# Unread matrix products of 512 columns in place of 128, three more groups of them, and a weight piece issued between the decayed keys of units 2 and 3

## The chip, the cores and the metric

The kernel runs on one core of a Trainium2 chip. Five engines work on their own instruction streams and wait for each other through semaphores: TensorE (PE, matrix products; its weight loads are listed apart as PEld), VectorE (DVE), ScalarE (ACT), GpSimd (POOL) and SyncE (SP). Transfers between memory and the chip are issued by SP, ACT or POOL and run on 16 DMA engines that they share. The metric is the device time of one execution in microseconds; lower is better.

## The reference

A lightning-attention step with a decay per head is followed by a two-layer network with a leaky activation. Four sequences, 8 heads, 768 positions, 64 dimensions a head; the network has 512 inputs, 2048 hidden units and 3072 tokens. In blocks of positions:

```python
intra = (q_b @ k_b.T * Dmask) @ v_b
inter = (q_b * lam_pow) @ kv_state
out   = intra + inter
kv_state = lam_block * kv_state + (k_b * rev_pow).T @ v_b

h = x @ w_in
g = max(h, 0) + alpha * min(h, 0)
y = g @ w_out
```

All inputs and the output are float32; the kernel computes the products in float16 with float32 accumulation.

## The kernel before, in words

The tokens are cut into six chunks `c` of 512 (two sequences by 256 positions). A chunk's attention is done in four **units** (`bi` of two sequences, `hh` of two halves of the heads), numbered through: units 0 to 3 belong to chunk 0. The order of every engine's instructions is written out by hand as a long list of calls (L766 to L1159); no scheduler moves anything. Each engine executes its own calls in that order. PE's stream starts with the list's first call to `fill`.

The steps of one unit `n`, with the engine that does each:

- `cast` (L411) and `key_decayed` (L432) read the raw key tile: a float16 copy, and the keys times their decay, two operations each. The letter names the engine (A for ACT, V for DVE, G for POOL).
- `turn` (L446): 12 transposes on PE into the PSUM tile `tp`, which has a single buffer (tag `tk`). `turned` (L464) copies `tp` to `qkT` on ACT or DVE; the next `turn` needs that copy done.
- `decayed` (L478) multiplies the turned queries by their decay, giving `qdT`.
- `cluster(old, new)` (L500) is one dense run on PE: products of the old unit's `qdT` with the state R (L532), 16 scores `s` of the new unit (L580), the old unit's outputs from `sm` and `v` (L552), and 16 state products of the new unit (L597).
- `masked` (L608) multiplies scores by the decay mask on DVE, giving `sm`. `aged` (L673) on POOL and `state` (L653) on ACT or DVE advance the state R.
- `out_of` (L632) copies the finished output to `xT`, the input of the network.

The network's steps are `up` (L694: four products with columns of `w_in` into a PSUM bank), `below` (L707, a relu on ACT into `m`), `gate` (L712, DVE combines `m` and the bank into `g`) and `down` (L726). Three PSUM banks take turns (slots 0, 1, 2); an `up` into a slot waits until the gate before it has read that slot.

`fill(n)` (L376) issues n products of a constant 128x128 tile with itself into slot 2. Nothing reads them; they keep PE at work where its next input isn't there yet. There are eight calls, 122 products in all: 50, 4, 6, 2, 28, 16, 2, 14 (in the order of the list), each 128 columns wide, and the last of them ends before 20 us.

`load_win(c0, n)` (L115) has POOL issue the transfer of n columns of `w_in`, cast to float16 on the way. The piece of columns 1024 to 1535 is issued after `decay_mask(0)` and before the decayed keys of units 2 and 3. The `up` steps 8 to 11 of chunk 0 read it.

Of the kernel before, what the change touches and what calls it, by code (L numbers as in the profile page):

```python
# [11 lines left out]
def kernel(  # L12
# [16 lines left out]
    nc = tc.nc  # L29
    ctx.enter_context(tc.manual_schedule())  # L30
    fp32 = mybir.dt.float32
# [14 lines left out]
    CH = 2 * W  # L46
# [11 lines left out]
    ps = ctx.enter_context(tc.tile_pool(name="ps", bufs=1, space=bass.MemoryType.PSUM))  # L58
# [56 lines left out]
    def load_win(c0, n):  # L115
        nc.gpsimd.dma_start(
            out=w_in_sb[:, :, ds(c0, n)],
            in_=moe_w_in[:, ds(c0, n)].rearrange("(g p) f -> p g f", p=128),
        )
# [34 lines left out]
    filler = const.tile([128, 128], fp16, name="filler")  # L154
# [82 lines left out]
    def mask_of(hl, hh):  # L237

        m = dmask[:, hl, ds(2 * hh, 2)]
        x = [list(y) for y in m.ap]  # L240
        return bass.AP(tensor=m.tensor, offset=m.offset, ap=[x[0], x[1], [64, 2], [1, L]])
# [10 lines left out]
    def mask_log(hp):  # L252

        m = MK[hp] = bank(hp % 2, "mk_ps")
        nc.tensor.matmul(
            m[:, 0:384].rearrange("p (h x) -> p h x", h=2),
            lhsT=ident,
            rhs=drop.unsqueeze(1).to_broadcast([128, 2, 192]),
            start=True,
            stop=False,  # L260
            skip_group_check=True,
        )
        for hl in range(2):
            h = 4 * (hp // 2) + hp % 2 + 2 * hl
            log = parts[:, h : h + 1]
            for lhsT, rhs in ((log.to_broadcast([128, L]), col16[:, 0:192]), (row16, log.to_broadcast([128, 192]))):
                nc.tensor.matmul(  # L267
                    m[:, ts(hl, 192)],
                    lhsT=lhsT,
                    rhs=rhs,  # L270
                    start=False,
                    stop=(lhsT is row16),
                    skip_group_check=True,
                )
# [8 lines left out]
    def key_logs():  # L283
        nc.vector.tensor_tensor(
            out=klog,
            in0=loglam.unsqueeze(2).to_broadcast([128, H, 2]),
            in1=rev_f.unsqueeze(1).to_broadcast([128, H, 2]),
            op=ALU.mult,
        )
# [76 lines left out]
    def bank(slot, name):  # L366
        return ps.tile([128, CH], fp32, tag=f"b{slot}", name=name)

    def slopes(slot):
        at = bank(slot, "at_ps")  # L370
        nc.tensor.transpose(at[:, 0:NF], alpha_sb, ident32)
        nc.vector.tensor_scalar(
            out=oma, in0=at[:, 0:NF], scalar1=-1.0, scalar2=1.0, op0=ALU.mult, op1=ALU.add
        )

    def fill(n):  # L376

        t = bank(2, "op_fill")
        for _ in range(n):
            nc.tensor.matmul(t[:, 0:128], lhsT=filler, rhs=filler, start=True, stop=True)  # L380


# [15 lines left out]
    def engine(x):  # L398
        return nc.vector if x == "V" else nc.gpsimd

    def view(t, hh):
        return t[:, ds(4 * hh, 4), :].rearrange("p h (e d) -> p e h d", e=2)
# [8 lines left out]
    def cast(n, x, eng):  # L411
        c, bi, hh = units[n]
        t = T.setdefault(n, {})
        if (c, bi) in Q16 and x == "q":
            out = view(rows16(x, c, bi), hh)
        elif (c, bi) in Q16:
            out = t["k16"] = half_pool.tile([128, 2, 4, D], fp16, tag="k16", name="k16", bufs=4)
        else:
            if "qk16" not in t:
                t["qk16"] = half_pool.tile([128, 2, 2, 4, D], fp16, tag="qk16", name="qk16")  # L420
            out = t["qk16"][:, int(x == "k")]
        if (c, bi) in Q16 and x == "q":
            copy_on(eng, out, view(raws[c, bi, x], hh))
        else:

            copy_on(
                eng,
                out.rearrange("p e s d -> p s e d"),
                raws[c, bi, x][:, ds(4 * hh, 4), :].rearrange("p (hl hp) ed -> p hp hl ed", hp=2),
            )  # L430

    def key_decayed(n, eng="G"):  # L432
        c, bi, hh = units[n]
        kr = view(raws[c, bi, "k"], hh)
        kdec = half_pool.tile([128, 2, 4, D], fp16, tag="kdec", name="kdec", bufs=4)
        for e in range(2):
            decay = kdecay[:, ds(4 * hh, 4), e] if c < FIRST else nkdecay[:, ds(4 * hh, 4)]
            engine(eng).tensor_tensor(  # L438
                out=kdec[:, e],
                in0=kr[:, e],  # L440
                in1=decay.unsqueeze(2).to_broadcast([128, 4, D]),
                op=ALU.mult,
            )
        T.setdefault(n, {})["kdec"] = kdec
# [163 lines left out]
    def masked(n, hl=None):  # L608
        t = T[n]
        hh = units[n][2]  # L610
        if hl is not None:
            t.setdefault("sm", {})[hl] = sm_pool.tile([128, 2, 2, L], fp16, tag=f"sm{hl}", name=f"sm{hl}")
            nc.vector.tensor_tensor(  # L613
                out=t["sm"][hl],
                in0=t["s"][:, hl].rearrange("p (h x j) -> p h x j", h=2, x=2),
                in1=mask_of(hl, hh),
                op=ALU.mult,
            )
        else:

            t["sm"] = sm_pool.tile([128, 2, 2, L], fp16, tag="sm0", name="sm0")
            nc.vector.tensor_tensor(
                out=t["sm"],
                in0=t["s"][:, :, 0 : 4 * N].rearrange("p l (e x) -> p l e x", e=2),
                in1=nmask[:, ds(4 * hh, 4)]
                .rearrange("p (l h) j -> p l (h j)", l=2)
                .unsqueeze(2)
                .to_broadcast([128, 2, 2, 2 * N]),
                op=ALU.mult,
            )  # L630
# [13 lines left out]
    def follows(n, a):  # L644

        c, bi, hh = units[n]
        step = L // N if c < FIRST else 1
        b, i = 2 * (c % 2) + bi, 4 * (c // 2) + a * step
        if (b, hh, i + step) not in R:
            state_tile(b, hh, i + step)  # L650
        return R.get((b, hh, i)), R.get((b, hh, i + step))

    def state(n, a):  # L653
        before, then = follows(n, a)
        c, bi, hh = units[n]
        if then is None:
            return
        if c >= FIRST:
            for hp in range(2):
                nc.vector.scalar_tensor_tensor(  # L660
                    out=then[:, hp, :],
                    in0=before[:, hp, :],
                    scalar=nrdecay[:, 2 * hh + hp : 2 * hh + hp + 1],
                    in1=T[n]["kv"][a % 2][:, a // 2, hp, :],
                    op0=ALU.mult,
                    op1=ALU.add,
                )
        elif before is None:
            nc.scalar.activation(then, T[n]["kv"][a][:, 0], AF.Copy)  # L669
        else:  # L670
            nc.vector.tensor_tensor(out=then, in0=T[n]["kv"][a][:, 0], in1=T[n]["old", a], op=ALU.add)  # L671

    def aged(n, a):  # L673

        before, then = follows(n, a)
        if then is None:
            return
        hh = units[n][2]
        x = T.setdefault(n, {})["old", a] = half_pool.tile([128, 2, D], fp32, tag=f"old{a}", name=f"old{a}", bufs=4)
        nc.gpsimd.tensor_tensor(  # L680
            out=x,
            in0=before,
            in1=rdecay[:, ds(2 * hh, 2)].unsqueeze(2).to_broadcast([128, 2, D]),
            op=ALU.mult,
        )
# [8 lines left out]
    def up(c, f, bi, slot):  # L694
        n = CH if bi is None else W
        h_ps = HP[c, f, bi] = bank(slot, "h_ps")
        for gi in range(NHP):
            x = XT[c][:, gi]
            nc.tensor.matmul(  # L699
                h_ps[:, 0:n] if bi is None else h_ps[:, 0:n].rearrange("p (e j) -> p e j", e=2),  # L700
                lhsT=w_in_sb[:, gi, ts(f, 128)],
                rhs=x.rearrange("p e b j -> p (e b j)") if bi is None else x[:, :, bi, :],
                start=(gi == 0),
                stop=(gi == NHP - 1),
            )
# [84 lines left out]
    load16("v", 0, 1)  # L790
    slopes(1)
    key_logs()
    mask_log(2)
    cast(0, "k", "V")
    load_win(0, 256)
# [25 lines left out]
    aged(0, 1)  # L821
    turn(1)
    decay_mask(0)
    load_win(1024, 512)
    state(0, 1)
    fill(28)
    turned(1, "A")
    masked(0, 0)
    key_decayed(2, "G")
    masked(0, 1)  # L830
    cast(2, "k", "A")
    decayed(1, "V")
# [40 lines left out]
    state(3, 0)  # L873
    gate(0, 1, 0)
    aged(3, 1)
    cluster(3, None)
    load_win(1536, 512)
    state(3, 1)
    up(0, 2, 0, 2)
    out_of(3, "A")  # L880
    up(0, 3, 0, 0)
# [408 lines left out]
```

## Time and profile before

| What | us |
|---|---|
| median of three runs | 220.22 (219.63 to 220.26) |
| the profiled execution, its own time | 219.79 |
| its span, first to last instruction | 218.0 |
| DVE busy | 126.9 |
| ACT busy | 111.4 |
| POOL busy | 97.4 |

The profile is one execution. A line names the source line, the engine, the operation, the tile it writes and the tiles it reads, and the count; "idle before" is how long the engine stood still before it, with what ended the wait. "issue" stands for a wait that nothing in the profile ended. A product's recorded end is modelled, and products overlap in PE's pipeline, so the distance from start to start tells more than a single length. The chain of waits goes back from the last instruction, at each step to what released it.

### The profile page before, as it was taken

The page shows a single profiled execution, that of the slowest core. Times are in us where ns is not written, and L with a number is a line of the kernel's source. Part 1 is how long each engine was busy: PE and PEld are TensorE (multiplying, and loading weights), DVE is VectorE, ACT ScalarE, POOL GpSimd, SP SyncE. Part 2 cuts the span into 40 slices and gives each one's busy share as a digit, 9 for nine tenths or more (in the row PEclk, how much of TensorE's full clock was granted, in tenths as well). Part 3 has the DMA queues.
Part 4 walks back from the last instruction along what each step waited for, and adds up shares of the span by engine and source line. Part 5 has one row for each costly group of instructions (what it writes and reads, how often), then busy time and mean ns, then how long its engine had stood idle before and what let it go on. Part 6 is the DMA issues. An engine that isn't in the chain of part 4 may idle for free.

```text
span 218.0 us, 5901 instructions
## 1 busy us (share of the span) xinstructions
PE 209.7 (96%) x2463; PEld 112.9 (52%) x2463; DVE 126.9 (58%) x260; ACT 111.4 (51%) x209; POOL 97.4 (45%) x154
## 2 busy tenths in 40 slices
PE   8888899899999999999999999999999999999993
PEld 8677544656765545454444444444444444444452
DVE  3988786776787786554766666646755254444000
ACT  4762775834666565546565555555445434443121
POOL 7874797655988680875597352720200000000000
PEclk9999999999999999999999999999999999999999
DMA  4999899999998398499369998227011011101212
GB/s 117 248 193 226 195 164 182 202 210 198 308 218 214 74 226 93 96 186 155 87 64 220 192 229 133 69 80 70 29 51 48 6 46 48 48 8 43 96 52 94
DMA packets 71195, 28.45 MB, mean 130 GB/s; under 512 B 52080, under 2 KB 68224, under 8 KB 71168
## 3 DMA queue, kind: packets, MB, share of 16 engines
q0 software_dynamic: 26592, 8.65, 35.6%
q1 hardware_dynamic: 40800, 13.11, 31.0%
q10 hardware_dynamic: 3776, 6.31, 8.7%
q8 instruction: 19, 0.31, 0.6%
q14 instruction: 8, 0.07, 0.1%
HBM read 27.28 MB, written 6.29 MB: 154 GB/s over the span
## 4 chain that ended last, share of the span: by engine, by line
PE 91%; ACT 2%; DVE 2%; issue 2%; POOL 2%; ACTq 0%; POOLq 0%
PE h_ps L699 37%; PE o_ps L732 32%; PE o_ps L754 6%; PE acc L532 3%; PE s L580 2%; PE op_fill L380 2%; PE acc L552 2%; PE tp L460 2%; PE tp L455 1%; PE acc L597 1%; ACT qkT L392 1%; PE mk_ps L267 1%; ACT xT L392 1%; POOL vh L83 0%; ACT m L710 0%
## 5 line engine op out<-in xcount | busy, mean ns | idle before, releaser
L722 DVE SCALAR_TENSOR_TENSOR g<-m,oma,h_ps 128x512 f16<-128x512 f32 (+1 forms) x106 | 73.0, 696 | 64.1 <-ACT m L710 62.8
L699 PE MATMUL h_ps<-xT,w_in_sb 128*128 128x512 f16 (+1 forms) x424 | 96.7, 359 | 0.5 <-DVE g L722 0.2
L710 ACT ACTIVATE m<-h_ps 128x512 f32<-128x512 f32 (+1 forms) x106 | 58.8, 556 | 56.3 <-PE h_ps L699 54.7
L732 PE MATMUL o_ps<-w_out_sb,g 128*128 128x512 f16 x320 | 81.2, 379 | 0.0
L699 PEld LDWEIGHTS <-w_in_sb 128*128 128x128 f16 x424 | 39.6, 98 | 40.6 <-issue 1.4
L732 PEld LDWEIGHTS <-g 128*128 128x128 f16 x320 | 30.9, 98 | 35.8
L743 ACT ACTIVATE o_sb<-o_ps 128x512 f32<-128x512 f32 (+2 forms) x25 | 14.5, 580 | 18.8 <-PE o_ps L754 11.0
L613 DVE TENSOR_TENSOR sm<-s,dmask 128x512 f16<-128x512 f32 x32 | 21.2, 683 | 1.8 <-PE s L580 1.8
L392 ACT ACTIVATE xT<-acc 128x512 f16<-128x512 f32 x22 | 13.1, 597 | 16.5 <-PE acc L552 9.4
L680 POOL TENSOR_TENSOR old<-R,rdecay 128x128 f32<-128x128 f16 x24 | 9.6, 408 | 26.5 <-DVE R L671 16.0
L438 POOL TENSOR_TENSOR kdec<-kraw,kdecay 128x256 f16<-128x256 f32 x30 | 18.5, 645 | 0.6 <-ACT kdecay L292 0.5
L488 POOL TENSOR_TENSOR qdT<-qkT,nqdecay 128x512 f16<-128x512 f16 x8 | 9.4, 1169 | 20.8 <-DMA qkT<-qk 17.7
L488 POOL TENSOR_TENSOR qdT<-qkT,qdecay 128x512 f16<-128x512 f16 (+1 forms) x12 | 12.0, 1003 | 4.8 <-DVE qkT L394 3.1
L754 PE MATMUL o_ps<-w_out_sb,g 128*128 128x512 f16 (+2 forms) x80 | 14.0, 336 | 0.0
L532 PE MATMUL acc<-qdT,R 64*64 64x64 f16 (+1 forms) x216 | 10.9, 217 | 0.9 <-ACT R L669 0.7
L380 PE MATMUL op_fill<-filler 128*128 128x128 f16 x122 | 10.3, 252 | 1.1 <-DVE sel L203 1.1
L532 PEld LDWEIGHTS <-R 64*64 64x64 f16 x224 | 5.9, 104 | 9.5 <-issue 6.4
L754 PEld LDWEIGHTS <-g 128*128 128x128 f16 x80 | 7.2, 98 | 6.9
L660 DVE SCALAR_TENSOR_TENSOR R<-R,nrdecay,s 128x64 f16<-128x64 f16 x48 | 10.5, 275 | 0.0
L580 PE MATMUL s<-qkT 64*64 64x128 f16 (+1 forms) x384 | 9.3, 210 | 0.9 <-issue 0.5
L380 PEld LDWEIGHTS <-filler 128*128 128x128 f16 x122 | 9.0, 116 | 1.6 <-DVE sel L203 1.1
L438 POOL TENSOR_TENSOR kdec<-kraw,nkdecay 128x256 f16<-128x256 f32 x16 | 9.5, 612 | 0.0
(98 smaller groups left out, 159.5 us busy)
## 6 DMA issues: line engine op xcount, KB each, us to landing
out_dram<-o_sb ACTq DMA_DIRECT2D x23, 256.0 KB, 2.2
kraw<-in_k_dram SPq DMA_DIRECT2D x12, 256.0 KB, 5.2
kraw<-in_k_dram SPq DMA_DIRECT2D x6, 512.0 KB, 7.3
qraw<-in_q_dram SPq DMA_DIRECT2D x10, 256.0 KB, 6.4
vh<-in_v_dram POOLq DMA_DIRECT2D x8, 256.0 KB, 8.8
w_out_sb<-in_moe_w_out_dram POOLq DMA_DIRECT2D x4, 512.0 KB, 8.0
w_in_sb<-in_moe_w_in_dram POOLq DMA_DIRECT2D x3, 512.0 KB, 10.2
qh<-in_q_dram POOLq DMA_DIRECT2D x5, 256.0 KB, 8.3
```

Source lines behind the costliest of these rows:

```text
L380: nc.tensor.matmul(t[:, 0:128], lhsT=filler, rhs=filler, start=True, stop=True)
L392: nc.scalar.activation(out, in_, AF.Copy)
L438: engine(eng).tensor_tensor(out=kdec[:, e], in0=kr[:, e], in1=decay.unsqueeze(2).to_broadcast([128, 4, D]), op=ALU.mult,)
L488: engine(eng).tensor_tensor(out=out, in0=src, in1=(qdecay if c < FIRST else nqdecay)[:, hh].rearrange("p e h j -> p (e h) j").unsqueeze(2) ...
L532: nc.tensor.matmul(o, lhsT=before[ds(hl * 64, 64), hp, :], rhs=x, start=not own and e == 0, stop=False, skip_group_check=True,)
L613: nc.vector.tensor_tensor(out=t["sm"][hl], in0=t["s"][:, hl].rearrange("p (h x j) -> p h x j", h=2, x=2), in1=mask_of(hl, hh), op=ALU.mult,)
L699: nc.tensor.matmul(h_ps[:, 0:n] if bi is None else h_ps[:, 0:n].rearrange("p (e j) -> p e j", e=2), lhsT=w_in_sb[:, gi, ts(f, 128)], rhs=x ...
L710: nc.scalar.activation(m[:, 0:n], HP[c, f, bi][:, 0:n], AF.Relu, scale=-1.0)
L722: nc.vector.scalar_tensor_tensor(out=g, in0=mv, scalar=oma[:, f : f + 1], in1=hv, op0=ALU.mult, op1=ALU.add)
L732: nc.tensor.matmul(O[c, t], lhsT=G[c, f][:, t // 2, t % 2, :], rhs=w_out_sb[:, f, :], start=(f == 0), stop=(f == NF - 1),)
L743: nc.scalar.activation(o_sb[:, 0:n], o_ps[:, 0:n], AF.Copy)
L754: nc.tensor.matmul(o_ps[:, 0:n], lhsT=G[c, f][:, t // 2, t % 2, :], rhs=w_out_sb[:, f, ds(c0, n)], start=(f == 0), stop=(f == NF - 1),)
```

## The change

`fill` issues one product of 512 columns for every four asked for (the constant tile read four times over as the moving operand) and narrow ones for the remainder; it can write to the `tk` buffer instead of slot 2. Three calls are new: `fill(4)` behind `key_logs`, `fill(8, True)` ahead of `cluster(3, None)`, and `fill(4, True)` between `state(3, 1)` and the up step behind that cluster. The piece `load_win(1024, 512)` moves on POOL behind the two operations of `key_decayed(2, "G")` and ahead of the two of `key_decayed(3, "G")`.

The 122 narrow products become 28 wide and 10 narrow ones, and the new calls add four wide ones: PE's stream is 80 products and 80 weight loads shorter. On DVE, ACT and SP the order is unchanged, on POOL only the piece moves.

```diff
-    def fill(n):
-
-        t = bank(2, "op_fill")
-        for _ in range(n):
+    def fill(n, other=False):
+
+        if other:
+            t = ps.tile([128, CH], fp32, tag="tk", name="tk_fill")
+        else:
+            t = bank(2, "op_fill")
+        wide = filler.unsqueeze(1).to_broadcast([128, 4, 128])
+        for _ in range(n // 4):
+            nc.tensor.matmul(t.rearrange("p (x j) -> p x j", x=4), lhsT=filler, rhs=wide, start=True, stop=True)
+        for _ in range(n % 4):
             nc.tensor.matmul(t[:, 0:128], lhsT=filler, rhs=filler, start=True, stop=True)
...
     slopes(1)
     key_logs()
+    fill(4)
     mask_log(2)
...
     decay_mask(0)
-    load_win(1024, 512)
     state(0, 1)
     fill(28)
     turned(1, "A")
     masked(0, 0)
     key_decayed(2, "G")
+    load_win(1024, 512)
     masked(0, 1)
...
     aged(3, 1)
+    fill(8, True)
     cluster(3, None)
     load_win(1536, 512)
     state(3, 1)
+    fill(4, True)
     up(0, 2, 0, 2)
```

## The prediction

> **What bounds the kernel now.** I read the page first, then the chain of waits, then the first 28 us on each engine in order of time.
>
> ```profile
> span 218.0 us, 5901 instructions
> ...
> PE 209.7 (96%) x2463; PEld 112.9 (52%) x2463; DVE 126.9 (58%) x260; ACT 111.4 (51%) x209; POOL 97.4 (45%) x154
> ...
> q8 instruction: 19, 0.31, 0.6%
> ...
> PE 91%; ACT 2%; DVE 2%; issue 2%; POOL 2%; ACTq 0%; POOLq 0%
> ...
> w_in_sb<-in_moe_w_in_dram POOLq DMA_DIRECT2D x3, 512.0 KB, 10.2
> ```
>
> TensorE (PE) carries 91% of the chain that ends last. One row of that chain, the first long stretch of up products, shows how dense it is from there on:
>
> ```profile
> 27.10 7.97 PE h_ps L699 x36
> ```
>
> 36 products of 512 columns take 7.97 us, 0.221 us each, without a hole. Behind 27.10 us the order on all engines is unchanged, so what reaches 27.10 us reaches the end. What the change is worth is decided before that, where PE still waits. PE in order of time (start, length, work, in brackets the idle time before it and what ended it):
>
> ```profile
> 1.09 5.09 PE L380 MATMUL op_fill<-filler 128*128 128x128 f16 x50 [1.09 <-DVE sel L203]
> ...
> 11.52 0.39 PE L455 MATMUL tp<-ident,k 128*128 128x128 f16 x4
> ...
> 12.19 1.74 PE L380 MATMUL op_fill<-filler 128*128 128x128 f16 x28
> ...
> 14.41 0.30 PE L597 MATMUL h_acc<-vh,kdec 64*64 64x64 f16 x11
> 15.32 0.23 PE L597 MATMUL h_acc<-vh,kdec 64*64 64x64 f16 x5 [0.61 <-issue]
> 15.48 0.40 PE L455 MATMUL tp<-ident,k 128*128 128x128 f16 x4
> ...
> 16.16 1.07 PE L380 MATMUL op_fill<-filler 128*128 128x128 f16 x16
> 17.06 0.39 PE L455 MATMUL tp<-ident,k 128*128 128x128 f16 x4
> ...
> 17.95 0.46 PE L580 MATMUL s<-qkT 64*64 64x128 f16 x16
> ...
> 18.25 0.46 PE L552 MATMUL acc<-sm,vh 64*64 64x128 f16 x16
> 18.50 0.34 PE L597 MATMUL acc<-vh,kdec 64*64 64x64 f16 x16
> 18.77 0.95 PE L380 MATMUL op_fill<-filler 128*128 128x128 f16 x14
> 19.78 0.60 PE L699 MATMUL h_ps<-xT,w_in_sb 128*128 128x256 f16 x4
> ...
> 20.32 0.40 PE L580 MATMUL s<-qkT 64*64 64x128 f16 x9
> 21.25 0.30 PE L580 MATMUL s<-qkT 64*64 64x128 f16 x7 [0.53 <-issue]
> ...
> 21.89 0.61 PE L699 MATMUL h_ps<-xT,w_in_sb 128*128 128x256 f16 x4
> 23.15 0.55 PE L532 MATMUL acc<-qdT,R 64*64 64x128 f16 x4 [0.65 <-ACT R L669]
> ...
> 23.85 1.49 PE L699 MATMUL h_ps<-xT,w_in_sb 128*128 128x256 f16 x12
> 25.52 9.56 PE L699 MATMUL h_ps<-xT,w_in_sb 128*128 128x256 f16 x48 [0.18 <-DVE g L722]
> ```
>
> Twice PE stops in the middle of a run of equal products, at 15.32 and at 21.25, and no engine or transfer of data ends the wait ("issue"). The reader is to see where: in busy time per stretch (the first bracketed count is PE's products, the second its weight loads)
>
> ```profile
> 0.00:10.15 10.15, 8.35 (x94) 7.40 (x95) 5.84 (x23) 6.26 (x14) 8.16 (x20) 1.00 0.88 182
> 0.00:14.80 14.80, 12.91 (x222) 11.35 (x223) 10.12 (x30) 9.57 (x20) 11.96 (x26) 1.00 1.12 184
> 14.80:20.80 6.00, 5.33 (x128) 4.24 (x128) 5.08 (x11) 1.98 (x6) 2.87 (x7) 1.00 1.27 207
> ```
>
> the first stop comes after 222 products, the second exactly 128 products and 128 loads later: 256 instructions. The page's instruction queue moved 19 packets, 16 KB each, and PE's 2 x 2463 instructions over 19 are 259. One of these packets started here (DMA of 12.75 to 12.85 us):
>
> ```profile
> q8 instruction: 1, 0.02, 60.1%
> ```
>
> So I read the two stops as late code: PE reaches the end of a block of 256 instructions before the next one is usable. The packet of 12.8 us is followed by the restart at 15.32; the earlier boundary, product 94, was passed at 10.15. A block thus took 5.2 us from there, and the second at most 5.9 us (15.32 to 21.25).
>
> The Trainium skill, page "Runtime: NRT & Kernel Launch", section "Instruction fetch mechanics", also has blocks of 16 KiB or 256 instructions, but holds the cost of crossing one to be mostly hidden. By that rule the two stops would be something else and would stay (a rival below); the spacing of exactly 256 in the rows speaks for the blocks and against "hidden" here.
>
> **Part 1: fewer, wider unread products.** PE runs 80 products and 80 loads fewer in all: 36 in the first group, 21, 12 and 9 in the groups of 28, 16 and 14, 3 in each of the groups of 4 and 6, less 4 new ones. In time this is almost nothing: 16 narrow ones last from 16.16 to 17.06, 56 ns each, four of them 0.225 us against 0.221 for a wide one. That is 0.03 us on the 28, 0.02 on the 16, 0.01 on the 14: I count 0.05 up to the turn of unit 3. The first 50 run at 100 ns each (5.02 us to the following work), nearly half speed, though the clock column reads 1.00; 6,400 columns are 6,400 columns either way, so I take zero there (bounds: nothing, or the clock released later, a rival).
>
> What counts is where the boundaries fall. Ahead of the old boundary at product 222 stand 62 products fewer, and 12 more go before the next, so product 222 of the new program is number 296 of the old one, amid the 18.25 row; its predecessor moves to number 135, the 11.52 row; and the one after falls on the row of 25.52. New spacings in time, with the stops taken out: from 11.5 to 17.5, 6.0 us against 5.2 needed in the first case; from 17.5 to about 24.6, 7.1 against 5.9. Both blocks then come in time, with 0.8 and 1.2 us to spare.
>
> What the stops cost: from 14.41 to 15.48 there are 1.07 us for 16 state products, which take 0.27 at 18.50 to 18.77: **0.80 us**. Nine scores take 0.93 us at 20.32 to 21.25, where 16 need 0.30 (17.95 to 18.25): **0.75 us**.
>
> **Part 2: the moved weight piece.** Without the first stop the turn of unit 3 (17.06) must still wait for the copy of unit 2's turn on VectorE (DVE), and that stands in this queue:
>
> ```profile
> 13.45 1.88 DVE L488 TENSOR_TENSOR qdT<-qkT,qdecay 128x256 f16<-128x256 f16 x1
> 15.25 0.68 DVE L613 TENSOR_TENSOR sm<-s,dmask 128x512 f16<-128x512 f32 x1
> 16.27 0.69 DVE L394 COPY qkT<-tp 128x1024 f16<-128x1024 f16 x1 [0.34 <-PE tp L460]
> ...
> 20.83 0.48 DVE L722 SCALAR_TENSOR_TENSOR g<-m,oma,h_ps 128x256 f16<-128x256 f32 x1 [0.37 <-ACT m L710]
> ```
>
> The qdT multiply lasts 1.88 us. On GpSimd (POOL) meanwhile:
>
> ```profile
> 11.54 0.39 POOL L680 TENSOR_TENSOR old<-R,rdecay 128x128 f32<-128x128 f16 x1 [0.82 <-ACT R L669]
> 11.89 0.80 POOL L116 DMA_DIRECT2D w_in_sb<-in_moe_w_in_dram  x1
> 12.71 2.33 POOL L438 TENSOR_TENSOR kdec<-kraw,kdecay 128x256 f16<-128x256 f32 x4
> ```
>
> Four key multiplies run from 12.71 to 15.04, and the DVE multiply ends 0.29 us after the last. It is held by them. In the new order POOL runs two (0.58 each) from 11.89 to 13.05, writes the piece until 13.85, then the other two until 15.0. The DVE multiply becomes ready at 13.45, inside the 0.8 us of the piece. Its own length without POOL isn't in these rows; between 0.29, its remainder behind POOL, and 1.88 I take 0.4, since it reads and writes half the elements of the 0.68 and 0.69 us operations. It ends by 13.9, masking follows at 14.3 when the scores are there, and the copy at 15.4, 0.1 behind its transposes. So the 0.80 passes on whole.
>
> The Trainium skill, "SBUF — State Buffer", section "SBUF: two separate sides", says that DVE operations with two SBUF inputs and GpSimd share a port pair, held for one whole instruction, and that GpSimd can't write descriptors while it is locked out. By that the DVE multiply would have got in after the first POOL multiply, at 13.3 or 13.9; the row shows it only after the last, so I go by the row.
>
> The piece itself is issued 1.1 us later. It takes 10.2 us to land, so until about 24.1; its columns are read from the 17th product behind 27.10 on, at 30.6, some 29.5 in the new program. That cover hides it. The keys of unit 3 end when they did.
>
> **Part 3: the three new groups.** The four after the key logs (one wide product, 0.22) stand in front of mask products that wait for DVE's log parts; nothing. The eight before the last unit's output (0.44) stand in the 0.65 us that PE waits for R at 23.15; nothing. The four behind it stand directly before the up product of 23.85, whose relu is next on ScalarE (ACT):
>
> ```profile
> 22.53 0.39 ACT L710 ACTIVATE m<-h_ps 128x256 f32<-128x256 f32 x1
> 22.81 0.28 ACT L669 ACTIVATE R<-h_acc 128x128 f16<-128x128 f32 x1
> ...
> 23.97 0.60 ACT L392 ACTIVATE xT<-acc 128x512 f16<-128x512 f32 x1 [0.88 <-PE acc L552]
> 24.57 1.19 ACT L710 ACTIVATE m<-h_ps 128x256 f32<-128x256 f32 x3
> ```
>
> ACT is free at 24.57, when that product is done too (23.85 and the 0.60 of the same shape at 19.78, then the way over), so the wide one delays relu, gate and the row of 25.52 by its **0.22 us**.
>
> **The sum.** Turn of unit 3 earlier by 0.80 + 0.05 = 0.85; with the second stop 1.60. Then a new limit: the up product of 21.89 must wait until DVE has gated its bank (20.83 + 0.48 = 21.31, now 20.46), so it starts at 20.5, 1.37 earlier, 0.23 lost. ACT's m and R and the wait at 23.15 move by the same amount. Less 0.22 that is 1.15, and I take **1.1 us**. On the profiled execution (219.79, of it 218.0 span) that makes 218.7; on the median of the runs shown (220.22, from 219.63) 219.1. I take **219.0**, nearer the median.
>
> **Rivals.**
> - The multiply on DVE stays held, because it comes after 13.85 or because writing descriptors holds it too. For: no row shows such a multiply beside a piece being issued. Against: 0.4 us of room. Then masking ends at 15.93, the copy at 16.62, the turn of unit 3 starts at 16.7 instead of 16.2: 0.47 lost, 219.5.
> - The change doesn't remove the stops (not code, or each recurs as long elsewhere). For: the later blocks are to be fetched over a DMA at a share above 1.2. Against: the spacing of 256. Left are 0.05 of gain and 0.22 of cost: 220.3.
> - Slower: the first new boundary's block arrives yet later. It is asked for when the 11.52 row runs, and the moved piece is put into the DMA queues beside it. PE wants it at 17.5, so it decides from 18.6 us on, where the 1.1 are gone, 7.1 us after asking; every further us is a us. At 8 us, half as long again as the 5.2 of this boundary before, 221.1.
> - Slower in a smaller way: wide products release the clock later. At half speed each us of PE work behind 6.1 us costs another; two us, less the saving, 221.
>
> **Chances.** Forecast 0.55; held multiply 0.15; stops stay 0.14; late block 0.09; late clock 0.07. A change below 0.3% (0.66 us) can't be told from none here. The forecast is faster in nine of ten of its cases, the held multiply in under half: faster 0.57; the two slower rivals and a few of the stops that stay: slower 0.17; same 0.26. The forecast's own range is 218.4 to 219.7 (spread of the runs, and 0.2 on the sum). For 8 in 10 it must reach the stops that stay and touch the slower cases: 218.2 to 220.8.
>
> **What would show it.** Right: no "issue" idle above 0.2 us on PE before 27 us; qdT of unit 1 near 0.4 us, inside the piece's issue; the turn of unit 3 near 16.2; the up product of 21.89 near 20.5, waiting for the gate; the row of 27.10 near 26.0. Wrong: an "issue" idle at a new place inside the outputs of unit 1 (about 17.5 us), a qdT above 1 us, 100 ns products beyond 6.1 us, or a hole behind 27 us that eats the gain, above all before the down products that wait for transfers.

## The result, and the profile after

| | before | after |
|---|---|---|
| median of 16 runs each, us | 220.25 (219.42 to 221.06) | 219.28 (218.52 to 219.75) |
| the profiled execution, us | 219.79 | 218.56 |
| its span, us | 218.0 | 216.8 |

The ratio is 0.9946, 95% interval 0.993 to 0.9962: faster by 0.97 us. The forecast was 219.0.

The page of the changed kernel, the lines that answer to those of before:

```profile
span 216.8 us, 5741 instructions
...
PE 209.9 (97%) x2383; PEld 107.8 (50%) x2383; DVE 126.0 (58%) x260; ACT 111.7 (52%) x209; POOL 97.1 (45%) x154
...
q8 instruction: 18, 0.29, 0.6%
...
PE 91%; ACT 2%; DVE 2%; POOL 2%; issue 1%; ACTq 0%; POOLq 0%
```

PE is busy as long as before with 80 products fewer; the instruction queue moves one packet less; "issue" falls from 2% of the chain to 1%. PE in order of time:

```profile
14.34 0.34 PE L603 MATMUL h_acc<-vh,kdec 64*64 64x64 f16 x16
14.61 0.40 PE L461 MATMUL tp<-ident,k 128*128 128x128 f16 x4
...
16.16 0.39 PE L461 MATMUL tp<-ident,k 128*128 128x128 f16 x4
...
19.39 0.46 PE L586 MATMUL s<-qkT 64*64 64x128 f16 x16
...
20.44 0.60 PE L705 MATMUL h_ps<-xT,w_in_sb 128*128 128x256 f16 x4 [0.16 <-DVE g L728]
...
21.68 0.55 PE L538 MATMUL acc<-qdT,R 64*64 64x128 f16 x4 [0.21 <-ACT R L675]
...
22.39 0.39 PE L384 MATMUL tk_fill<-filler 128*128 128x512 f16 x1
22.61 1.47 PE L705 MATMUL h_ps<-xT,w_in_sb 128*128 128x256 f16 x12
24.27 3.90 PE L705 MATMUL h_ps<-xT,w_in_sb 128*128 128x256 f16 x22 [0.18 <-DVE g L728]
```

The 16 state products (14.34) and the 16 scores (19.39) run through; both "issue" stops are gone. The turn of unit 3 starts at 16.16 instead of 17.06, 0.90 earlier. The up product that started at 21.89 starts at 20.44, 1.45 earlier, and now the gate ends its wait. The up product of 23.85 starts at 22.61, 1.24 earlier. The row of 27.10 in the chain that ends last is now:

```profile
25.85 7.97 PE h_ps L705 x36
```

It is 1.25 earlier with the same length, and that is the difference of the two profiled times (219.79 less 218.56 is 1.23).

### The profile page after: what moved, and what is told of

It is laid out like the page before. It is cut to its first block, busy times and chain, and to the rows that moved or that the text cites. A ratio compares the mean times of both kernels' runs of the same rounds, so it can differ in the third digit from the quotient of the medians.

```text
span 216.8 us, 5741 instructions
## 1 busy us (share of the span) xinstructions
PE 209.9 (97%) x2383; PEld 107.8 (50%) x2383; DVE 126.0 (58%) x260; ACT 111.7 (52%) x209; POOL 97.1 (45%) x154
## 4 chain that ended last, share of the span: by engine, by line
PE 91%; ACT 2%; DVE 2%; POOL 2%; issue 1%; ACTq 0%; POOLq 0%
PE h_ps L705 38%; PE o_ps L738 32%; PE o_ps L760 6%; PE acc L538 3%; PE s L586 2%; PE acc L558 2%; PE op_fill L384 2%; PE tp L466 2%; PE tp L461 1%; PE acc L603 1%; ACT qkT L398 1%; ACT m L716 1%; PE mk_ps L267 1%; DVE g L728 1%; POOL vh L83 0%
## 5 line engine op out<-in xcount | busy, mean ns | idle before, releaser
L398 ACT ACTIVATE xT<-acc 128x512 f16<-128x512 f32 x22 | 13.1, 597 | 16.5 <-PE acc L558 9.5
L384 PE MATMUL op_fill<-filler 128*128 128x512 f16 x29 | 9.5, 466 | 1.1 <-DVE sel L203 1.1
L558 PE MATMUL acc<-sm,vh 64*64 64x128 f16 (+1 forms) x352 | 8.4, 209 | 0.0
```

The lines of the kernel that those rows point to most:

```text
L384: nc.tensor.matmul(t.rearrange("p (x j) -> p x j", x=4), lhsT=filler, rhs=wide, start=True, stop=True)
L398: nc.scalar.activation(out, in_, AF.Copy)
```

## The experiments

Each kernel differs from the kernel before or from the changed one by the few lines shown. The kernel before had medians of 220.14 (35 runs beside the first four experiments) and 220.27 (29 runs beside the last four). A profile is one execution, and single executions of one kernel differ by 0.7 us and more: of the 16 of the changed kernel six lie between 218.52 and 218.75 and ten between 219.26 and 219.75. What parts the two groups isn't shown. So rows are compared at the place of the edit, and medians with their intervals.

**Wide products alone.** The kernel before with the new body of `fill`; no moved piece, no new groups.

```diff
-        for _ in range(n):
+        wide = filler.unsqueeze(1).to_broadcast([128, 4, 128])
+        for _ in range(n // 4):
+            nc.tensor.matmul(t.rearrange("p (x j) -> p x j", x=4), lhsT=filler, rhs=wide, start=True, stop=True)
+        for _ in range(n % 4):
             nc.tensor.matmul(t[:, 0:128], lhsT=filler, rhs=filler, start=True, stop=True)
```

> The kernel before, with only the unread products widened (8 calls); none of the three new groups, and the weight piece of columns 1024 to 1535 issued where it was. Theory (late code): PE's 256-instruction boundaries fall on other instructions, so both 'issue' stops before 27 us are gone; the qdT multiply of unit 1 on DVE still lasts about 1.9 us behind four key multiplies on POOL, so the turn of unit 3 starts near 16.7 and not 16.2 us. Nothing stands before the up product at 23.85, so 0.2 us more is kept: 0.6 to 0.9 us faster than before. Rival (the stops are not code and the gain comes from the moved piece): both stops stay and the time is that of before within 0.2 us.

Median 219.88 (218.74 to 221.02, 12 runs), ratio 0.9984 (0.9954 to 1.0014). PE and DVE in order of time:

```profile
16.81 0.40 PE L461 MATMUL tp<-ident,k 128*128 128x128 f16 x4
18.77 0.38 PE L461 MATMUL tp<-ident,k 128*128 128x128 f16 x4 [0.25 <-DVE qkT L400]
```
```profile
15.64 1.88 DVE L494 TENSOR_TENSOR qdT<-qkT,qdecay 128x256 f16<-128x256 f16 x1
```

Both stops are gone here too. In place of the first, PE waits for the copy behind the held multiply: from one turn to the next it takes 1.96 us (16.81 to 18.77), against 1.55 in the changed kernel (14.61 to 16.16), so 0.41 is lost. This profile is a weak test of the blocks, since its clock was halved for a while and its code had more time. The 0.6 to 0.9 us that were expected aren't in the median, which is 0.26 below that of the kernel before with an interval that holds no change at all. Five of the 12 runs had the halved clock. The other seven have a median of 219.48, against 219.83 for the 26 of the kernel before with a mean clock of 0.997 or more; and the two quickest, 218.74 and 218.78, are 0.5 below its quickest (219.26).

**All unread products narrow.** The changed kernel, piece and groups as they are, with 128 columns each.

```diff
-        for _ in range(n // 4):
+        for _ in range(0):
...
-        for _ in range(n % 4):
+        for _ in range(n):
```

> The changed kernel with every unread product narrow again (the three new groups too, as 4, 8 and 4 narrow ones; the piece stays moved). Theory (late code): ahead of product 222 stand only 4 products more than before, so both stops come back, the first among the state products or outputs of unit 0 near 14.4 us, the second 128 products later near 20 us, each 0.5 to 0.8 us long; freeing the DVE multiply (about 0.5 us long) brings nothing, since PE stands still anyway; 0.0 to 0.4 us slower than before. Rival (the piece or the new groups bring the gain): 0.8 us or more faster than before.

Median 220.21 (219.34 to 220.32, 12 runs), ratio 0.9986 (0.9964 to 1.0008): the gain is gone. PE in order of time:

```profile
8.07 0.26 PE L267 MATMUL mk_ps<-col,parts 128*128 128x192 f16 x1 [1.53 <-DVE parts L250]
...
15.15 0.39 PE L603 MATMUL h_acc<-vh,kdec 64*64 64x64 f16 x16
15.48 0.40 PE L461 MATMUL tp<-ident,k 128*128 128x128 f16 x4
...
20.31 0.34 PE L586 MATMUL s<-qkT 64*64 64x128 f16 x5
21.21 0.36 PE L586 MATMUL s<-qkT 64*64 64x128 f16 x11 [0.56 <-issue]
```

The second stop is back. Of the first only 0.06 us is left, in the state products that hold product 222 (15.15 to 15.48, 0.33 us, against 0.27 in the changed kernel). The log parts came 0.74 us late in this execution (8.07 against 7.33 in the changed kernel's profile), so PE came that much later to the boundary, while the instruction packet ran at 13.0, 0.2 later than before: the block was there almost as soon as PE wanted it. In the median, the moved piece and the new groups without the wide products bring nothing that can be told from none.

**The piece at its old place.** The changed kernel otherwise.

```diff
     decay_mask(0)
+    load_win(1024, 512)
...
     key_decayed(2, "G")
-    load_win(1024, 512)
```

> The changed kernel with the weight piece issued where it was, ahead of both pairs of decayed keys. Theory: no stops, but the qdT multiply of unit 1 on DVE lasts until POOL's four key multiplies are through (about 15.3 us), the turn of unit 3 starts near 16.7 instead of 16.16 us, and 0.4 to 0.6 us of the gain is lost: 0.5 to 0.8 us faster than before. Rival (the place of the piece does not matter): as fast as the changed kernel, 1.0 to 1.2 us faster than before.

Median 219.71 (218.99 to 220.32, 12 runs), ratio 0.9961 (0.9938 to 0.9984). PE, then DVE:

```profile
14.62 0.40 PE L461 MATMUL tp<-ident,k 128*128 128x128 f16 x4
16.59 0.38 PE L461 MATMUL tp<-ident,k 128*128 128x128 f16 x4 [0.25 <-DVE qkT L400]
...
62.65 0.39 PE L738 MATMUL o_ps<-w_out_sb,g 128*128 128x512 f16 x1 [0.81 <-issue]
```
```profile
13.44 1.89 DVE L494 TENSOR_TENSOR qdT<-qkT,qdecay 128x256 f16<-128x256 f16 x1
```

Busy time in a stretch from the start (the stretch, its length, busy time and count of PE, PEld, DVE, ACT and POOL, granted clock, DMA share, GB/s):

```profile
0.00:62.40 62.40, 58.69 (x862) 34.59 (x862) 45.88 (x101) 37.43 (x78) 45.64 (x78) 1.00 1.28 208
```

With four key multiplies in one row the DVE multiply takes 1.89 us again, and the turn of unit 3 starts at 16.59 instead of 16.16. This 0.43 is what the moved piece is worth once the first stop is gone, and the medians, though not of one series, differ by as much (219.71 and 219.28). The stop at 62.65 is of the execution, not of the edit: PE's stream is that of the changed kernel, whose profile doesn't have it. It lies behind 862 products, which is 222 and five times 128, and an instruction packet ran at 60.1, so it is a late block again.

**The first group narrow.** The changed kernel with its first 50 unread products of 128 columns: 36 products more ahead of everything, the rest wide.

```diff
-    fill(50)
+    fill(50, width=1)
```

The new argument, whose few lines are left out here, has `fill` issue narrow products alone.

> The changed kernel with only the first group narrow again: 50 products of 128 columns for 12 wide and 2 narrow ones, the same 6400 columns in the same 5 us, but 36 products more ahead of everything. Theory (late code): the boundaries move 36 products up: to about 10.5, 16.5 and 21.8 us instead of 11.5, 17.4 and 24.5. The middle block has 6.0 us as before and comes in time; the next has only 5.3 us, against 5.9 to 6.7 that blocks have taken here, so a stop of 0.5 to 1.4 us appears at the products with R before the outputs of unit 3, where there was none in either kernel. 0.5 us faster to 1.0 us slower than before, and 0.5 us or more slower than the changed kernel. Rival (the number of instructions ahead does not matter): as fast as the changed kernel, no stop.

Median 220.01 (219.05 to 220.39, 12 runs), ratio 0.9979 (0.9956 to 1.0002). Busy time in stretches (columns as above), then PE in order of time:

```profile
0.00:16.50 16.50, 14.52 (x223) 10.91 (x223) 11.08 (x33) 10.45 (x23) 13.02 (x28) 1.00 1.15 185
0.00:21.95 21.95, 19.29 (x350) 14.28 (x351) 15.93 (x44) 12.81 (x30) 15.09 (x33) 1.00 1.16 196
0.00:66.00 66.00, 62.24 (x990) 40.30 (x990) 47.02 (x106) 39.62 (x83) 48.53 (x81) 1.00 1.30 210
```
```profile
22.00 0.54 PE L538 MATMUL acc<-qdT,R 64*64 64x128 f16 x4 [0.51 <-ACT R L675]
...
66.47 0.21 PE L603 MATMUL acc<-vh,kdec 64*64 64x64 f16 x1 [0.49 <-issue]
```

PE passes product 222 by 16.5 us and then stands at 350 until 22.00. ACT wrote R at 21.37 here and at 21.36 in the changed kernel, where the same products start at 21.68: the trace puts the wait down to R, but the last 0.32 of it is the block, wanted 5.2 us after the one ahead and there after 5.5. Its packet ran at 19.6, 2.4 ahead of the restart. A second stop follows behind 990 products, 222 and six times 128. The products that stop are the same as ever; only the count ahead of them changed. (The medians agree in sign, 220.01 against 219.28; the stop at 990 needn't come in every execution.)

**Without the group behind the key logs.** The changed kernel otherwise.

```diff
     key_logs()
-    fill(4)
```

> The changed kernel without the first new group (four unread products behind the key logs); all else as changed. Theory: that group, which the prediction counted as nothing, keeps PE from standing still for 1.5 us ahead of the mask products in the executions whose log parts come late, and so keeps the clock from being halved for 3.4 us. Without it some executions (9 of 35 of the kernel before, 5 of 12 of the kernel with wide products alone) show a mean clock of 0.992 again and take about 1 us more: three groups of times near 218.6, 219.3 and 220.3 to 220.9, two to five of twelve in the last, median 219.3 to 219.5, mean 0.3 to 0.5 above that of the changed kernel. Rival (the group is worth nothing and the 0.992 executions were of the chip's making): times of 218.5 to 219.7 only, median 219.28, no clock below 0.995.

Median 219.07 (218.53 to 220.81, 12 runs), ratio 0.9942 (0.9918 to 0.9965). One execution of twelve had the clock of 0.992 (220.81), where two to five were expected, and the median isn't above that of the changed kernel. The theory missed; by this experiment alone, one run is too few for the rival to be refused either (the last section counts all runs).

**That group alone.** The kernel before with four narrow unread products behind the key logs.

```diff
     key_logs()
+    fill(4)
```

> The kernel before with nothing but the first new group (four narrow unread products behind the key logs). Theory: no execution with a clock below 0.995, so none near 221; the two lower groups of times of the kernel before stay, near 219.6 and 220.3, because both code stops stay (they move by four products); median 219.9 to 220.2, highest below 220.6. Rival (group worth nothing): two to four of twelve executions near 221.0 with a clock of 0.992, as before.

Median 219.82 (219.19 to 221.31, 12 runs), ratio 0.9989 (0.9966 to 1.0011); two executions at 221.03 and 221.31 with clocks of 0.992 and 0.990. So the group by itself doesn't always keep the clock from being halved, and the theory fell as it stood. Both stops stood, four products earlier in their rows. The second:

```profile
21.02 0.36 PE L580 MATMUL s<-qkT 64*64 64x128 f16 x11 [0.55 <-issue]
```

The nine scores ahead of it became five, since four more products stand ahead of them: the stop goes with the count and not with the work.

**Without the last group.** The changed kernel without the four products ahead of the up step of 22.61.

```diff
     state(3, 1)
-    fill(4, True)
     up(0, 2, 0, 2)
```

> The changed kernel without the group of four between the last unit's state and the up step behind it. Theory (the prediction's term of 0.22 us): that up product starts 0.22 us earlier, the relu behind it starts at 23.1 instead of 23.32, and everything from 23.85 of the changed kernel on is 0.2 us earlier: 218.35 for the executions that were at 218.55, median 219.0 to 219.1. Rival (ScalarE is no earlier ready, the term is nothing): median 219.28, relu at 23.3.

Median 218.86 (218.32 to 219.11, 6 runs), ratio 0.9931 (0.9907 to 0.9956). PE, ACT and DVE in order of time:

```profile
22.39 1.49 PE L705 MATMUL h_ps<-xT,w_in_sb 128*128 128x256 f16 x12
24.05 4.34 PE L705 MATMUL h_ps<-xT,w_in_sb 128*128 128x256 f16 x24 [0.18 <-DVE g L728]
28.79 3.40 PE L705 MATMUL h_ps<-xT,w_in_sb 128*128 128x512 f16 x15 [0.40 <-DVE g L728]
```
```profile
23.10 1.19 ACT L716 ACTIVATE m<-h_ps 128x256 f32<-128x256 f32 x3
```
```profile
26.37 1.71 DVE L400 CAST k<-kraw 128x512 f16<-128x512 f32 x1
```

In the changed kernel the relu stood so:

```profile
23.32 1.19 ACT L716 ACTIVATE m<-h_ps 128x256 f32<-128x256 f32 x3 [0.21 <-PE h_ps L705]
```

Without the group the up step starts at 22.39, the relu at 23.10 instead of 23.32 and without a wait, the next row at 24.05 instead of 24.27: the 0.22 of the prediction, to the hundredth. The two quickest executions, 218.32 and 218.36, lie where they were expected (218.35). The profiled execution lost it again at 28.79, to a cast on DVE (last section). This is the lowest median measured, but its interval overlaps that of the changed kernel; that it is faster than that one is shown in the rows, not in the times.

**The moved piece alone.** The kernel before with the piece moved.

```diff
     decay_mask(0)
-    load_win(1024, 512)
...
     key_decayed(2, "G")
+    load_win(1024, 512)
```

> The kernel before with nothing but the moved piece. Theory: the DVE multiply of unit 1 takes 0.57 us instead of 1.88, but the first code stop still holds unit 2's turn until 15.5, so the turn of unit 3 stays at 17.06 and the times are those of the kernel before: ratio 1.000 within its interval, groups near 219.6, 220.3 and 221.0. Rival 1 (the piece has a gain of its own): the 0.4 us that taking it back lost in the changed kernel come here too, median 219.7. Rival 2 (the later piece delays code blocks): the restarts at 15.32 and 21.25 come later, median above 220.4.

Median 221.11 (219.56 to 222.61, 12 runs), ratio 1.0026 (1.0 to 1.0051). DVE in order of time, then the granted clock (the column 1.00 or 0.50) in two stretches:

```profile
15.74 0.57 DVE L488 TENSOR_TENSOR qdT<-qkT,qdecay 128x256 f16<-128x256 f16 x1
```
```profile
5.53:8.94 3.41, 1.92 (x27) 1.30 (x25) 3.10 (x11) 2.26 (x4) 2.71 (x4) 1.00 1.41 251
8.94:12.35 3.41, 3.41 (x29) 2.67 (x30) 1.64 (x3) 1.56 (x4) 1.93 (x3) 0.50 1.56 220
```

The multiply is free, as expected. The second stop stands (0.56 us, up to 22.76); the first doesn't, since the halved clock brought PE to product 222 only at 16.8, so this profile can't show the piece beside the first stop. Nine of the 12 executions had a lowered clock (0.992, one 0.982), against eight of the 29 of the kernel before beside them, so the median says nothing of the piece. The three others, 219.56, 219.78 and 220.26, lie where the kernel before has its own with a full clock (219.46 to 220.50). That the piece gains nothing while the first stop stands fits them, but three runs don't show it. The lowered clock of this execution isn't the doing of the piece: the clock falls at 8.94, and POOL issues the piece at 15.3.

## Why the prediction was right, point by point

**Late code.** Right, and shown from both sides: narrow products bring a stop back, and stops move with the count of products ahead (onto the last unit's output with the first group narrow, four earlier with four more). Over the whole of all ten profiles PE has eight "issue" idles above 0.15 us, at products 222, 350, 862 and 990, and one more stop at 350 that the trace puts down to R (the first group narrow): all nine at 222 plus a multiple of 128. Each ends 2.3 to 2.5 us behind a packet of the instruction queue, the two of before 2.5 (12.8 to 15.32) and 2.4 (18.9 to 21.25). The room was smaller than forecast. In the changed kernel, busy time in stretches, and the queue that carried code in the stretches 14.6 to 14.7 and 21.6 to 21.7 us:

```profile
0.00:17.45 17.45, 15.71 (x221) 8.88 (x225) 12.07 (x36) 10.45 (x23) 12.99 (x28) 1.00 1.15 188
...
0.00:24.50 24.50, 22.09 (x350) 13.28 (x351) 17.06 (x47) 14.54 (x34) 17.59 (x37) 1.00 1.16 206
```
```profile
q8 instruction: 1, 0.02, 60.9%
...
q8 instruction: 1, 0.02, 63.0%
```

PE wants the two blocks right behind 17.45 and 24.50, as forecast (17.5 and 24.6). Their packets ran at 14.6 and 21.6. With the 2.5 us of the first stop of before, an estimate, these blocks were usable near 17.1 and 24.1, with 0.3 to 0.4 us to spare where the prediction had 0.8 and 1.2. What it mis-sized is the time from a boundary to the next block, which it took as fixed: the packet came 2.7 us after the boundary in the first case before (10.15 to 12.8) and 4.2 after it in the second case here (17.45 to 21.6). Over the ten profiles the first two packets ran 1.1 to 4.2 us after PE had passed their boundaries; what sets that time stays open. The rival of the late block was nearer than I took it for.

The Trainium skill, "Runtime: NRT & Kernel Launch", section "Instruction fetch mechanics", holds such crossings to be mostly hidden. The profile of the changed kernel agrees, with 18 packets and no stop; before, two stops of 0.80 and 0.75 us do not, nor does the idle of 0.81 at 62.65.

**The held multiply.** Right in kind: 0.57 us in place of 1.88, the turn of unit 3 at 16.16 (forecast 16.2), and 0.43 lost with the piece back (forecast 0.47). The 0.4 for the multiply was 0.17 too small, which did no harm because the copy still waits 0.40 us for its transposes. (The prediction took it as half the elements of both neighbours; it is half of the masking's 512 columns, but a quarter of the copy's 1024.) DVE, then POOL, in the changed kernel:

```profile
13.43 0.57 DVE L494 TENSOR_TENSOR qdT<-qkT,qdecay 128x256 f16<-128x256 f16 x1
...
15.40 0.69 DVE L400 COPY qkT<-tp 128x1024 f16<-128x1024 f16 x1 [0.40 <-PE tp L466]
```
```profile
11.89 1.18 POOL L444 TENSOR_TENSOR kdec<-kraw,kdecay 128x256 f16<-128x256 f32 x2
13.02 0.80 POOL L116 DMA_DIRECT2D w_in_sb<-in_moe_w_in_dram  x1
13.85 1.21 POOL L444 TENSOR_TENSOR kdec<-kraw,kdecay 128x256 f16<-128x256 f32 x2
```

The multiply ends at 14.00, 0.18 behind the issue of the piece and only 0.15 into the next key multiply. That the row of key multiplies held it is shown by the place of the piece alone: 1.88 or 1.89 us in all four profiles with four multiplies in a row, 0.57 in all six with the piece between them.

**The groups.** Eight ahead of the last output: free, and 0.21 of the wait for R is left. Four behind it: 0.22, shown by leaving them out. Four behind the key logs: nothing in the profile (the mask products start at 7.33 in both). In other executions they may be worth more than the nothing of the prediction (last section).

**The sum.** 0.85 for the turn of unit 3 was 0.90; 1.60 with the second stop was 1.69 at the tenth score (21.25 before; 19.39 and nine sixteenths of 0.30 after); the gate's limit took 0.24 (forecast 0.23) and left 1.45; the last group left 1.24. I took 1.1 from a sum of 1.15, and 1.23 came in the profiled pair, 0.97 in the medians. Neither is off by more than the spread of the runs. That the total comes so close is in part luck: the medians also hold executions with a halved clock (last section), which the sum doesn't have. The rival of the late clock fell with the first group: the work behind it starts at 5.96, before at 6.11.

## What to carry to other kernels

An "issue" idle in the middle of equal products, at the same count of instructions from the last one and shortly behind a packet of the instruction queue, was late code here: count products up to such an idle before looking for an engine. Unread products are then best issued wide, since they buy the same time for a quarter of the instructions; and behind a stop that goes, look for the next queue that was hidden by it, here a DVE operation held by a row of POOL operations.

## What the runs showed of the hardware that was not expected

- **A halved clock after a pause of PE.** In the profile of the wide products alone, log parts came at 8.07 and PE had stood still for 1.53 us; then the clock was halved for 3.41 us:

```profile
5.00:8.41 3.41, 1.69 (x12) 0.86 (x10) 2.98 (x10) 1.93 (x3) 2.82 (x4) 1.00 1.40 252
8.41:11.82 3.41, 3.41 (x29) 2.18 (x28) 1.39 (x4) 1.97 (x6) 2.36 (x3) 0.50 1.42 236
```

  PE was busy for 1.69 us of the stretch ahead (1.92 with the piece alone). With all products narrow the first 3.41 us at the full clock had 1.90, and nothing was halved behind them:

```profile
4.43:7.84 3.41, 1.90 (x27) 1.44 (x24) 2.46 (x6) 2.08 (x4) 3.38 (x5) 1.00 1.36 240
```

  So PE's busy time alone doesn't decide it. By the mean clock (0.992 or less), nine of 35 and eight of 29 executions of the kernel before were of this kind and none of the 16 of the changed kernel, so some of the gain in the median may be theirs: without its four times above 220.8 the kernel before of the first table has a median of 220.13, and the gain is 0.85. Counted over all kernels whose clocks are on record, 32 of 100 executions without the group behind the key logs had it and 2 of 70 with the group. So the group seems to have a part in it. The two pairs of kernels that differ in it alone don't show that by themselves (eight of 29 against two of 12, one of 12 against none of 16), and how it works stays open.
- **The same cast, 0.98 or 1.71 us.** A cast of DVE (0.42 us in the profile of before) stands beside POOL's key multiplies and the transfer that POOL issues after them. DVE and POOL in the changed kernel:

```profile
26.59 0.98 DVE L400 CAST k<-kraw 128x512 f16<-128x512 f32 x1
```
```profile
25.79 1.22 POOL L444 TENSOR_TENSOR kdec<-kraw,kdecay 128x256 f16<-128x256 f32 x2
26.92 1.14 POOL L83 DMA_DIRECT2D vh<-in_v_dram  x1
```

  and POOL without the last group, where the cast is ready 0.22 earlier and takes 1.71, until 28.08:

```profile
26.92 0.94 POOL L83 DMA_DIRECT2D vh<-in_v_dram  x1
```

  Behind the key multiplies either may go first. In the changed kernel the cast did, and the issue took 0.20 longer. Without the last group the issue did: the cast ended 0.22 behind it, and PE waited 0.40 us at 28.79, where it runs through in the changed kernel. The profile with the piece back has the second kind too, again with the cast ending 0.22 behind the issue:

```profile
27.01 1.51 DVE L400 CAST k<-kraw 128x512 f16<-128x512 f32 x1
```

  The execution without the last group took 218.91, 0.35 above the changed kernel's profiled one after being 0.22 ahead of it. So it seems that an issue of a transfer by POOL can hold a DVE operation too; no run changes this alone. The prediction priced that as a rival for the multiply of unit 1. There it did no harm, and whether 0.16 of the 0.57 us are such a hold (alone the multiply takes 0.41, and it ends 0.18 behind the issue) stays open. The Trainium skill, "SBUF — State Buffer", section "SBUF: two separate sides", has GpSimd not writing descriptors while DVE holds the shared ports. The 1.14 agrees, and so does the 1.03 of the profile with the first group narrow: in both the issue ends 0.49 us behind the cast. Where the cast was over within the first 0.38 us of the issue (all products narrow, and without the group behind the key logs), the issue kept its 0.94. The 1.51 and 1.71 are the reverse case, DVE behind an issue.
